# The second FFN's output product by Strassen's scheme, transposed, over two pairs of feature blocks at a time

## The chip, the cores and the metric

The kernel runs on one core of one Trainium2 chip. The metric is the device time of one execution in microseconds (us). Engines are named as in the profile: PE is the matmul engine and PEld its weight loads, DVE the vector engine, ACT the scalar engine, POOL GpSimd, SP the engine that issues the DMAs here.

## What is computed

Three steps in float32: banded attention, an FFN with a sigmoid gate on 2304 tokens, and a second FFN with separate gate and value products. Only the last one is changed.

```python
def _moe2_ref(x, w_gate, w_val, w_out):          # x: 2304 x 512
    g = x @ w_gate                               # 512 x 1536
    silu = g * (1.0 / (1.0 + np.exp(-g)))
    val = x @ w_val                              # 512 x 1536
    return (silu * val @ w_out).astype(np.float32)   # 1536 x 512
```

## The kernel before

Weights arrive as float64 words and are turned into two float32r halves, a high and a low part; activations are split the same way. Each product of 128x128 blocks is three matmuls (high by high, high by low, low by high).

**Order of the work.** The first 186 us or so are attention and the beginning of the first FFN, in an order written out by hand. Then the first FFN goes on over five blocks of tokens (`A_BLOCKS`) and 16 feature blocks, `h_part` and `y_part` in a loop over `idx`. Between those steps `advance(PACE[j])` runs some steps of `preparation`, which turns the second FFN's weights into the form in which they are used and writes them to scratch memory in HBM (`wscr`, `woscr`). The first FFN's result goes to `yscr` in HBM. The pools' slots and a scheduler with simulated time set the final order on each engine.

**The second FFN.** Tokens go in three groups `s` of 768, features in six pairs `p` of two 128-blocks: 18 pairs `q`, in the loop `for q in range(NQ)`. For each pair `gv_steps(q)` computes the gate (G) and the value (V) product by Strassen's scheme in Winograd's form: the matrices are cut in two by two quarters, and seven products of quarters (numbered 1 to 7) take the place of eight. A product (`product`) is 6 matmuls of 384 columns, and three PSUM banks collect them for each of G and V: `sx` takes products 1, 6, 7, 4 on top of each other, `sy` product 2, `sz` 5 and then 3. After 1, 5 and 6 ACT copies the bank (`keep_copy`, tile pc), after 2, 3 and 7 DVE adds a kept copy (`add`, tile c). `gate` then makes one quarter of silu(g)*v: tanh on ACT, two DVE operations, a copy to the high part on ACT and a subtraction for the low part on DVE (tile p).

`o_part(q, i)` multiplies tile i of 128 tokens of this result with the 256 rows of w_out that belong to the pair: 6 matmuls of 512 columns, of which the token tile is the stationary side, six such parts for a pair. The partial sums go to six accumulators in SBUF, by ACT for the first pair of a token group and by DVE (`acc`) for the others. The parts of pair q-1 run among the last products of pair q. `load_weights` brings the next pair's weights from scratch; its DMAs are issued by SP in order, each when the buffer it writes has been read for the last time. `y_steps` makes the seven sums of quarters of the activations for the next token group (tiles yr and ya), over the last two pairs of the group before, into the other one of two sets of buffers.

Of the kernel before, what the change touches and what calls it, by code (L numbers as in the profile page):

```python
# [26 lines left out]
PACE = {0: 1.4, 2: 2.0, 3: 2.2, 4: 2.3}  # L27

PAUSE = 77

PACE_LATE = 0.6
# [3 lines left out]
LATER = 2.5  # L35

SUPER = 6

O_ORDER = 3, 4, 5, 0, 1, 2

A_BLOCKS = (4, 2, 4, 4, 4)
# [40 lines left out]
def attention_two_ffn(ctx: ExitStack, tc: tile.TileContext, q, k, v, w_in, w_out, w_gate, w_val, w_out2, yscr, wscr, woscr, out):  # L82
# [9 lines left out]
    DM = out.shape[1]  # L92
# [25 lines left out]
    wpool = ctx.enter_context(tc.tile_pool(name="w", bufs=1, reuse_waits="tile"))  # L118
    cvp = ctx.enter_context(tc.tile_pool(name="cv", bufs=2))
# [114 lines left out]

    def fetch(slot, unit):

        m, p, h = unit
        pool, tag = slot()
        if m == "O":
            raw = pool.tile([P, 512, 2], U32, tag=tag, name="raw")  # L240
            src = w_out2[(2 * p + h) * P : (2 * p + h + 1) * P, :].bitcast(U32)
            nc.sync.dma_start(out=raw.rearrange("p c w -> p (c w)"), in_=src)
            return raw
        raw = pool.tile([P, 2, 2, P, 2], U32, tag=tag, name="raw")
        w = w_gate if m == "G" else w_val
        for f in range(2):
            src = w[2 * p + f].bitcast(U32).rearrange("p (a b c) -> p a b c", a=2, b=2)[:, :, h, :]
            nc.sync.dma_start(out=raw[:, f].rearrange("p a c w -> p a (c w)"), in_=src)
        return raw.rearrange("p f a c w -> p (f a c) w")

    def prepare(slot, raw, fetch_next, unit):

        m, p, h = unit
        cs = cvp.tile([P, 8, P], F32, tag="cv", name="cs")
        yield from fraction(raw, cs)
        fetch_next()
        if m == "O":
            pool, tag = slot()
            t = pool.tile([P, 1, 2, 512], F32R, tag=tag, name="wo")
            halves(t, slice(0, 1), cs.rearrange("p s c -> p (s c)")[:, :512].unsqueeze(1))  # L260
            nc.sync.dma_start(out=woscr[p][:, h * 1024 : (h + 1) * 1024], in_=flat(t))
            yield
            return
# [11 lines left out]
        at = wscr[p, "GV".index(m)]  # L275
        pool, tag = slot()
        wa = pool.tile([P, 4, 2, P], F32R, tag=tag, name="wa")
# [5 lines left out]
        wb = cvp.tile([P, 3, 2, P], F32R, tag="cv", name="wb")  # L283
# [317 lines left out]
    def y_part(j, f):  # L601
# [14 lines left out]
        for kk in range(KD):  # L616
            if j == len(a_blocks) - 1 and kk:
                yt = wpool.tile([P, TMAX * P], F32, tag=f"w{O_SLOTS - 1 + kk}", name="yt")
            else:
                yt = yo.tile([P, TMAX * P], F32, tag="yt", name="yt")  # L620
# [17 lines left out]
    def y_steps(s, tile_of):  # L638
# [3 lines left out]
        def quarter(i, j):  # L642
            t = yrp.tile([P, 2, HT], F32, tag="yr", name="yr")
# [13 lines left out]
        b11, b12, b22 = quarter(0, 0), quarter(0, 1), quarter(1, 1)  # L657
        split(1, b11)
        minus(b11, b12, b11)
        minus(b12, b22, b12)  # L660
# [3 lines left out]
        split(7, b12)  # L664
        b21 = quarter(1, 0)
        yield
        split(2, b21)
        split(6, b11)
        yield
        split(3, b22)  # L670
        minus(b11, b21, b11)
# [346 lines left out]
    for i in O_ORDER:  # L1018
        o_part(NQ - 1, i)
# [44 lines left out]
```

## Time and profile before

| what | value |
|---|---|
| median of 3 runs | 938.6 us (938.53 to 939.38) |
| the profiled execution's own time | 937.2 us |
| its span, first to last instruction | 935.4 us |
| PE busy | 916.7 us, 98% |
| DVE busy | 649.0 us, 69% |
| ACT busy | 422.0 us, 45% |
| second FFN, from its first matmul | from 517.4 us to the end |
| mean granted clock of TensorE | 0.994 |

The span is what the trace covers; 1.8 us of the execution's time lie outside it. Busy shares are averages over stages that differ; the second FFN is the stage that is changed most.

### The profile page before, as it was taken

How to read it: one execution, taken by the hardware profiler on the slowest of the kernel's cores; microseconds unless marked ns; L12 is line 12 of the kernel's file. 1: busy time of each engine (PE TensorE's matmuls, PEld its weight loads, DVE VectorE, ACT ScalarE, POOL GpSimd, SP SyncE). 2: the span in 40 equal slices, each digit the busy share in tenths (PEclk: the TensorE clock that was granted, in tenths of full speed). 3: DMA queues.
4: the chain of work that ended last, by engine and by line, in shares of the span. 5: the costliest groups of instructions: out<-in, count | busy, mean ns of one | idle time of the engine just before them, and what ended most of it. 6: DMA issues, size and time to landing. Idle time of an engine off the chain costs nothing.

```text
span 935.4 us, 15014 instructions
## 1 busy us (share of the span) xinstructions
PE 916.7 (98%) x5464; PEld 788.6 (84%) x5464; DVE 649.0 (69%) x1558; ACT 422.0 (45%) x968; POOL 123.6 (13%) x221
## 2 busy tenths in 40 slices
PE   6899999999999999999999999999999999999998
PEld 4577898787778877788888999999999999999996
DVE  7898797756876668757696567577545577545555
ACT  5565565643654446534454453344343343342321
POOL 4744004512331023300000000000000000000000
PEclk9899999999999999999999999999999999999999
DMA  8953202425543355435579488667765666766641
GB/s 319 358 200 134 93 13 62 151 93 166 176 150 128 126 195 192 139 108 191 196 267 325 166 333 322 226 211 265 265 209 203 208 255 220 275 213 216 212 151 67
DMA packets 62473, 182.38 MB, mean 195 GB/s; under 512 B 6080, under 2 KB 28096, under 8 KB 55488
## 3 DMA queue, kind: packets, MB, share of 16 engines
q1 hardware_dynamic: 62400, 181.43, 55.1%
q8 instruction: 43, 0.70, 0.3%
q14 instruction: 30, 0.25, 0.1%
HBM read 142.61 MB, written 38.80 MB: 194 GB/s over the span
## 4 chain that ended last, share of the span: by engine, by line
PE 86%; DVE 6%; DMA 3%; ACT 2%; POOL 1%; issue 1%; SPq 0%; DVEq 0%; POOLq 0%; ACTq 0%
PE sx L695 16%; PE o L765 16%; PE sz L695 8%; PE hp L561 6%; PE y L561 6%; PE hp L563 6%; PE y L563 6%; PE hp L562 6%; PE y L562 6%; PE sy L695 4%; PE xb L514 2%; PE sb L361 2%; PE pt L453 1%; DMA y_scratch<-yt 1%; DVE wraw L194 1%; POOL prob L421 1%
## 5 line engine op out<-in xcount | busy, mean ns | idle before, releaser
L695 PE MATMUL sx<-ya,wg 128*128 128x384 f32 x864 | 172.6, 336 | 0.0
L765 PE MATMUL o<-wo,p 128*128 128x512 f32 x648 | 158.9, 391 | 0.0
L695 PEld LDWEIGHTS sx<-ya,wg 128*128 128x128 f32 x864 | 153.1, 188 | 5.5 <-issue 0.3
L765 PEld LDWEIGHTS o<-wo,p 128*128 128x128 f32 x648 | 120.8, 188 | 21.4
L561 PE MATMUL hp<-xh,wt 128*128 128x512 f32 (+1 forms) x320 | 121.0, 378 | 0.5 <-DVE th L584 0.4
L563 PE MATMUL hp<-xh,wt 128*128 128x512 f32 (+1 forms) x320 | 118.1, 370 | 0.0
L562 PE MATMUL hp<-xl,wt 128*128 128x512 f32 (+1 forms) x320 | 118.0, 369 | 0.0
L562 PE MATMUL y<-gl,wt 128*128 128x512 f32 (+1 forms) x320 | 116.8, 371 | 0.5 <-DVE gl L592 0.5
L563 PE MATMUL y<-gh,wt 128*128 128x512 f32 (+1 forms) x320 | 117.0, 371 | 0.0
L561 PE MATMUL y<-gh,wt 128*128 128x512 f32 (+1 forms) x320 | 111.2, 377 | 0.2 <-DVE stat L386 0.2
L421 POOL TENSOR_SCALAR prob<-prob,stat 128x128 f32<-128x128 f32 x144 | 68.9, 498 | 204.4 <-DVE sb L331 55.7
L695 PE MATMUL sz<-ya,wg 128*128 128x384 f32 x432 | 84.1, 335 | 0.0
L592 DVE TENSOR_TENSOR gl<-th,gh 128x512 fp32r<-128x512 f32 (+1 forms) x80 | 52.4, 659 | 44.7 <-ACT gh L590 44.3
L590 ACT ACTIVATE gh<-th 128x512 fp32r<-128x512 f32 (+1 forms) x80 | 46.7, 586 | 78.5 <-PE y L563 55.2
L774 DVE SCALAR_TENSOR_TENSOR acc<-o,acc 128x512 f32<-128x512 f32 x90 | 61.4, 688 | 25.1 <-PE o L765 23.9
L695 PEld LDWEIGHTS sz<-ya,wg 128*128 128x128 f32 x432 | 75.8, 188 | 0.2
L716 DVE TENSOR_TENSOR c<-sy,pc 128x384 f32<-128x384 f32 x36 | 20.1, 558 | 79.5 <-PE sy L695 75.3
L561 PEld LDWEIGHTS hp<-xh,wt 128*128 128x128 f32 x320 | 60.4, 189 | 13.6 <-issue 1.6
L402 ACT ACTIVATE prob<-prob,stat 128x128 f32<-128x128 f32 x144 | 56.2, 392 | 34.4 <-DVE stat L386 34.3
L563 PEld LDWEIGHTS y<-gh,wt 128*128 128x128 f32 x320 | 60.3, 188 | 11.2 <-issue 1.0
L562 PEld LDWEIGHTS y<-gl,wt 128*128 128x128 f32 x320 | 60.3, 189 | 10.9 <-DVE gl L592 0.9
L563 PEld LDWEIGHTS hp<-xh,wt 128*128 128x128 f32 x320 | 60.2, 188 | 10.6
(90 smaller groups left out, 1385.6 us busy)
## 6 DMA issues: line engine op xcount, KB each, us to landing
wg<-w_scratch SPq DMA_DIRECT2D x36, 1024.0 KB, 6.9
wg<-w_scratch SPq DMA_DIRECT2D x36, 768.0 KB, 5.2
wo<-wo_scratch SPq DMA_DIRECT2D x18, 1024.0 KB, 6.9
w_scratch<-wa SPq DMA_DIRECT2D x24, 512.0 KB, 2.7
w_scratch<-wb SPq DMA_DIRECT2D x24, 384.0 KB, 3.5
wraw<-in_moe_w_in SPq DMA_DIRECT2D x16, 512.0 KB, 6.7
wraw<-in_moe_w_out SPq DMA_DIRECT2D x16, 512.0 KB, 7.3
raw<-in_moe_w_gate SPq DMA_DIRECT2D x24, 256.0 KB, 3.3
```

The costliest lines, as they stand in the source:

```text
L361: nc.tensor.matmul(out=sb[e][c : c + size, (i % 2) * 256 + lo : (i % 2) * 256 + hi], lhsT=u["q"][rows, i * P + c : i * P + c + size], rhs= ...
L402: nc.scalar.activation(out=prob[:, x], in_=prob[:, x], func=AF.Exp, bias=stat[:, 0, x : x + 1], scale=-1.0, accum_out=stat[:, 1, x : x + 1],)
L421: (nc.vector if (j, hp, g) in NORM_ON_VECTOR else nc.gpsimd).tensor_scalar(out=prob[:, x], in0=prob[:, x], scalar1=stat[:, 3, x : x + 1], ...
L561: nc.tensor.matmul(out=out_ap, lhsT=whi, rhs=xhi, start=start, stop=False)
L562: nc.tensor.matmul(out=out_ap, lhsT=whi, rhs=xlo, start=False, stop=False)
L563: nc.tensor.matmul(out=out_ap, lhsT=wlo, rhs=xhi, start=False, stop=stop)
L590: a = nc.scalar.activation(out=gh[:, :m], in_=th[:, :m], func=AF.Copy)
L592: d = nc.vector.tensor_tensor(out=gl[:, :m], in0=th[:, :m], in1=gh[:, :m].bitcast(F32), op=ALU.subtract)
L695: nc.tensor.matmul(out=bank_[:, :HT], lhsT=w[:, kk, at, a, :], rhs=y[:, b, kk, :], start=start and kk == 0 and n == 0, stop=kk == 1 and n ...
L716: marks["d"] = nc.vector.tensor_tensor(out=t, in0=b[:, :HT], in1=kept[m, k], op=ALU.add).ins
L765: nc.tensor.matmul(out=o, lhsT=ph[:, a, c], rhs=w[:, f, b, :], start=f == 0 and n == 0, stop=f == 1 and n == 2)
L774: nc.vector.scalar_tensor_tensor(out=acc, in0=o, scalar=0.5, in1=acc, op0=ALU.mult, op1=ALU.add)
```

## The change

**The output product.** `o_part` goes. `o_steps(q)` computes the output transposed (512 output rows by tokens; the host turns it back), with the weights as the stationary side and the gated activations moving. A group is two pairs, thus 512 features. For a group there are two calls, one for each `half` of the output rows, run during the two pairs after the group (the last group's two calls run at the end, interleaved). A call is again Strassen's seven products over three banks `ox`, `oy`, `oz`; a product is 6 matmuls of 384 columns, 3 with the pieces of each of the group's pairs. After each of the seven, the bank is added to an accumulator (DVE), or copied to it in a token group's first group of pairs for four of them (ACT).

**The pieces.** `pieces_of` takes the place of the end of `gate`: from the four gated quarters it makes the seven operands, four more subtractions on DVE, and splits each of the seven in a high and a low part (tile p, 24 buffers), where before there were four such splits.

**The weights of the output product** are prepared as those of G and V are: 8 steps for a unit in place of 4, seven quarters in place of four, and `load_weights` fetches two pieces of 1024 and 768 KB for each pair, where before it was one of 1024 KB. G's and V's weights move to a pool `kept` that shares its slots with four of the first FFN's weights.

**Around it.** `PACE` is higher, preparation rests at `REST`, goes on in the second FFN from its third pair at 0.8 steps a product, and the activations' sums for the next token group (`y_steps`) are made within one pair, into a single set of buffers.

```diff
-PACE = {0: 1.4, 2: 2.0, 3: 2.2, 4: 2.3}
-PAUSE = 77
-PACE_LATE = 0.6
+PACE = {0: 2.0, 2: 2.4, 3: 2.5, 4: 2.7}
+REST = 74
+LATE, PACE_LATE = 2, 0.8
...
+KEPT = 3, 5, 4, 6
+P_BUFS = 24
+O_STEPS = 1, 5, 6, 2, 7, 3, 4
...
-    def y_steps(s, tile_of):
+    def y_steps(s, tile_of, slot):
...
     def product(q, m, i, bank_, start):
         half, at = W_OF[i]
-        w, y = w2[q, m, half], y2[q // NP2, i]
+        w = w2[q, m, half]
         for kk in range(2):
             for n, (a, b) in enumerate(((0, 0), (0, 1), (1, 0))):
                 nc.tensor.matmul(
                     out=bank_[:, :HT],
                     lhsT=w[:, kk, at, a, :],
-                    rhs=y[:, b, kk, :],
+                    rhs=p2[2 * (q // 2 - 1) + kk, i][:, b, :] if m == "O" else y2[q // NP2, i][:, b, kk, :],
...
+        def split(i, src):
+            t = pp.tile([P, 2, HT], F32R, tag="p", name="p2", bufs=P_BUFS)
+            nc.scalar.activation(out=t[:, 0], in_=src, func=AF.Copy)
+            nc.vector.tensor_tensor(out=t[:, 1], in0=src, in1=t[:, 0].bitcast(F32), op=ALU.subtract)
+            p2[q, i] = t
...
+        def pieces_of(i):
+            gate(i)
+            if i == (0, 0):
+                split(1, b[i])
+            elif i == (1, 1):
+                split(3, b[i])
+            elif i == (0, 1):
+                b11, b12, b22 = b[0, 0], b[i], b[1, 1]
+                minus(b11, b12, b11)
+                split(5, b11)
+                minus(b12, b22, b12)
+                split(7, b12)
+                minus(b22, b22, b11)
+                split(6, b22)
+            else:
+                split(2, b[i])
+                minus(b[i], b[i], b[1, 1])
+                split(4, b[i])
...
-        for pair in ((1, 5), (2, 6), (3,), (7,), (4,)):
+        for pair in ((1, 5), (2, 6), (7,), (3,), (4,)):
...
-    def o_part(q, i):
-        p, s = q % NP2, q // NP2
-        w = w2[q, "O", 0]
-        o = bank("o")
-        c = slice(i * P, (i + 1) * P)
-        for f in range(2):
-            ph = p2[q][f]
-            for n, (a, b) in enumerate(((0, 0), (0, 1), (1, 0))):
-                nc.tensor.matmul(
-                    out=o, lhsT=ph[:, a, c], rhs=w[:, f, b, :], start=f == 0 and n == 0, stop=f == 1 and n == 2
-                )
...
+    def o_steps(q):
+
+        banks = {}
+        g, half = q // 2 - 1, q % 2
+        s, first, last = g // 3, g % 3 == 0, g % 3 == 2
+        for i in O_STEPS:
+            x = {1: "x", 6: "x", 7: "x", 4: "x", 2: "y", 5: "z", 3: "z"}[i]
+            new = x not in banks
+            if new:
+                banks[x] = bank("o" + x)
+            t = banks[x]
+            product(q, "O", i, t, new)
+            a, b = {1: (0, 0), 2: (0, 0), 6: (0, 1), 3: (0, 1), 5: (1, 1), 7: (1, 1), 4: (1, 0)}[i]
+            if first and i in (1, 5, 6, 4):
+                acc = pp.tile([P, HT], F32, tag=f"acc{half}{a}{b}", name="acc")
+                o2[half, a, b] = acc
+                nc.scalar.activation(out=acc, in_=t[:, :HT], func=AF.Copy, scale=0.5)
+            else:
+                acc = o2[half, a, b]
+                nc.vector.scalar_tensor_tensor(out=acc, in0=t[:, :HT], scalar=0.5, in1=acc, op0=ALU.mult, op1=ALU.add)
+            if last and i in (2, 3, 7, 4):
+                rows, cols = (2 * a + half) * P, s * SUPER * P + b * HT
+                nc.sync.dma_start(out=out[rows : rows + P, cols : cols + HT], in_=acc)
+            yield i
...
     for q in range(NQ):
         s, p = divmod(q, NP2)
-        if s + 1 < NS and p == NP2 - 2:
...
+        if s + 1 < NS and p == NP2 - 1:
+            pieces[s + 1] = y_steps(s + 1, piece, slot)
+        behind = o_steps(q) if q > 1 else iter(())
         for n, (m, i) in enumerate(gv_steps(q)):
...
+            if n % 2:
+                done = next(behind, None)
+                if done and q < NQ - 1:
+                    last_weights(q, done)
...
+    for _ in zip(o_steps(NQ), o_steps(NQ + 1)):
+        pass
```

**On PE**, in a pair near the end, before (tiles sx, sy, sz are the banks of G and V, o the bank of the output product, p_8884 and p_8885 the two feature blocks of the pair before):

```order
L695 MATMUL sz<-ya,wg 128x384 x12
L695 MATMUL sx<-ya,wg 128x384 x6
L765 MATMUL o<-wo,p_8884 128x512 x3
L765 MATMUL o<-wo,p_8885 128x512 x2
L695 MATMUL sx<-ya,wg 128x384 x6
L765 MATMUL o<-wo,p_8885 128x512
L765 MATMUL o<-wo,p_8884 128x512 x3
L765 MATMUL o<-wo,p_8885 128x512 x3
```

The same place with the change (ox, oy and oz are the output product's banks, the two tiles p pieces of the group's two pairs):

```order
L710 MATMUL sx<-ya,wg 128x384 x6
L710 MATMUL sz<-ya,wg 128x384 x6
L710 MATMUL oz<-p_9029,wg 128x384 x3
L710 MATMUL oz<-p_9252,wg 128x384 x3
L710 MATMUL sy<-ya,wg 128x384 x6
L710 MATMUL sx<-ya,wg 128x384 x6
L710 MATMUL ox<-p_9037,wg 128x384 x3
L710 MATMUL ox<-p_9260,wg 128x384 x3
```

The output product's matmuls now have the shape of G's and V's and stand after each second product of these, where before they had 512 columns and stood together in the second part of the pair.

**On DVE**, the end of a quiet pair before (c is `add`, th `gate`, p the low part, acc the output's accumulation):

```order
L716 TENSOR_TENSOR c_8980<-sz,pc 128x384
L725 SCALAR_TENSOR_TENSOR th_8982<-th_8982,c_8972 128x384
L716 TENSOR_TENSOR c_8994<-sx,pc 128x384
L726 TENSOR_TENSOR th_8982<-th_8982,c_8980 128x384
L725 SCALAR_TENSOR_TENSOR th_9004<-th_9004,c_8994 128x384
L729 TENSOR_TENSOR p_8884<-th_8982,p_8884 128x384
```

With the change (L734 is `minus` on the gated quarters, L739 the low part of a piece):

```order
L747 TENSOR_TENSOR th_9467<-th_9467,c_9465 128x384
L746 SCALAR_TENSOR_TENSOR th_9504<-th_9504,sx 128x384
L734 TENSOR_TENSOR th_9394<-th_9467,th_9394 128x384
L747 TENSOR_TENSOR th_9504<-th_9504,sx 128x384
L734 TENSOR_TENSOR th_9467<-th_9437,th_9467 128x384
L816 SCALAR_TENSOR_TENSOR acc<-ox,acc 128x384
L739 TENSOR_TENSOR p_9472<-th_9394,p_9472 128x384
L734 TENSOR_TENSOR th_9437<-th_9437,th_9394 128x384
L739 TENSOR_TENSOR p_9476<-th_9467,p_9476 128x384
```

Four L734 and three more L739 have come in for each pair.

**On SP**, before, the fourth quarter of the activations for the second token group (yr_6570) stands ahead of the second halves of the weights of pair 5:

```order
L684 DMA wg_6487<-w_scratch 128x2048 [waits DMAHW5_49,PE_49]
L684 DMA wg_6512<-w_scratch 128x2048 [waits DMAHW7_49,PE_49]
L645 DMA yr_6570<-y_scratch 128x2x384 [waits DVE_49]
L684 DMA wg_6578<-w_scratch 128x1536 [waits DMAHW6_49,DMAHW0_49,PE_49]
L684 DMA wg_6592<-w_scratch 128x1536 [waits DMAHW1_49,PE_49]
```

With the change it is issued in pair 5 (yr_6874), behind G's second half for pair 6 (wg_7022), which waits for the last product of G in pair 5:

```order
L699 DMA wg_6876<-w_scratch 128x2048 [waits DMAHW1_49,PE_49]
L699 DMA wg_6921<-w_scratch 128x2048 [waits PE_49]
L699 DMA wg_6931<-wo_scratch 128x2048 [waits PE_49]
L699 DMA wg_7022<-w_scratch 128x1536 [waits DMAHW4_49,PE_49]
L643 DMA yr_6874<-y_scratch 128x2x384 [waits DMAHW5_49,DVE_49]
L699 DMA wg_7050<-wo_scratch 128x1536 [waits DMAHW6_49,PE_49]
```

DVE meets this quarter behind the last gate of pair 5 (th2_7030):

```order
L747 TENSOR_TENSOR th2_7030<-th2_7030,sx_6811 128x384 [waits DVE_49]
L653 TENSOR_TENSOR yr_6821<-yr_6874,yr_6821 128x768 [waits DMAHW5_49,DVE_49]
L649 TENSOR_TENSOR ya_6904<-yr_6874,ya_6904 128x768 [waits Activation_49]
L734 TENSOR_TENSOR th2_6894<-th2_6993,th2_6894 128x384 [waits DVE_49]
L649 TENSOR_TENSOR ya_6982<-yr_6821,ya_6982 128x768 [waits Activation_49]
```

So the wait for the fourth quarter has moved from the next-to-last pair of a token group to the border of two groups, and pieces of pair 5 (L734) stand behind it on DVE.

## Rows read from the trace of the kernel before

**Rows 1.** The page's head, busy times, and the chain's share by engine.

```profile
span 935.4 us, 15014 instructions
...
PE 916.7 (98%) x5464; PEld 788.6 (84%) x5464; DVE 649.0 (69%) x1558; ACT 422.0 (45%) x968; POOL 123.6 (13%) x221
...
PE 86%; DVE 6%; DMA 3%; ACT 2%; POOL 1%; issue 1%; SPq 0%; DVEq 0%; POOLq 0%; ACTq 0%
```

**Rows 2.** Windows: us, busy time of each engine, PEclk, DMA share, GB/s.

```profile
350.00:375.00 25.00, 25.00 (x212) 18.70 (x215) 21.25 (x74) 15.46 (x51) 7.95 (x19) 1.00 0.51 179
...
475.00:500.00 25.00, 25.00 (x112) 20.67 (x112) 22.13 (x43) 12.66 (x23) 0.00 (x0) 1.00 0.76 270
...
517.40:935.40 418.00, 414.10 (x2173) 386.30 (x2171) 258.83 (x463) 151.88 (x299) 0.00 (x0) 1.00 0.64 225
```

**Rows 3.** The chain that ended last, 880 us to the end: start, us, what.

```profile
902.67 1.04 PE sx L695 x6
...
920.19 11.36 PE o L765 x50
...
931.57 0.69 DVE acc L774
```

**Rows 4.** Waits of PEld from 500 us on: us in total, times, longest.

```profile
PEld sx L695 <- issue: 0.3, 1, 0.3
```

**Rows 5.** The second FFN's window for the line L695 alone (PE, PEld).

```profile
517.40:935.40 418.00, 273.77 (x1512) 264.29 (x1511) 1.00 0.64 225
```

**Rows 6.** The same window for the line L765 alone.

```profile
517.40:935.40 418.00, 158.95 (x648) 120.79 (x648) 1.00 0.64 225
```

**Rows 7.** The line L695: duration in ns, least, median, most.

```profile
L695 PEld LDWEIGHTS sx<-ya,wg x864: 187/188/190, 517.2 to 919.7; 128*128 128x128 f32 x173
```

**Rows 8.** DVE's groups by shape in the second FFN: busy us, mean ns.

```profile
L774 DVE SCALAR_TENSOR_TENSOR acc<-o,acc 128x512 f32<-128x512 f32 x90 | 61.4, 688 | 25.1 <-PE o L765 23.9
L729 DVE TENSOR_TENSOR p<-th,p 128x384 fp32r<-128x384 f32 x72 | 39.9, 554 | 15.4 <-ACT p L728 15.4
...
L651 DVE TENSOR_TENSOR ya<-yr,ya 128x768 fp32r<-128x768 f32 x14 | 13.3, 950 | 0.0
```

**Rows 9.** DVE's timeline, 541 to 590 us: start, duration, instruction, idle before it.

```profile
557.06 0.55 DVE L725 SCALAR_TENSOR_TENSOR th<-th,sx 128x384 f32<-128x384 f32 x1 [2.18 <-ACT th L724]
557.71 0.55 DVE L726 TENSOR_TENSOR th<-th,sx 128x384 f32<-128x384 f32 x1
...
569.38 0.55 DVE L716 TENSOR_TENSOR c<-sz,pc 128x384 f32<-128x384 f32 x1
569.85 0.55 DVE L725 SCALAR_TENSOR_TENSOR th<-th,c 128x384 f32<-128x384 f32 x1
570.32 0.55 DVE L716 TENSOR_TENSOR c<-sx,pc 128x384 f32<-128x384 f32 x1
...
573.12 0.68 DVE L774 SCALAR_TENSOR_TENSOR acc<-o,acc 128x512 f32<-128x512 f32 x1
573.72 0.68 DVE L230 TENSOR_TENSOR wo<-cs,wo 128x512 fp32r<-128x512 f32 x1
```

**Rows 10.** ACT's groups by shape in the second FFN.

```profile
L728 ACT ACTIVATE p<-th 128x384 fp32r<-128x384 f32 x72 | 37.6, 522 | 63.2 <-DVE th L726 63.0
L711 ACT ACTIVATE pc<-sx 128x384 f32<-128x384 f32 x72 | 35.1, 488 | 64.1 <-PE sx L695 63.7
```

**Rows 11.** Windows of 6 us in the second FFN, columns as in Rows 2.

```profile
529.00:535.00 6.00, 5.96 (x34) 5.67 (x34) 5.80 (x13) 3.12 (x6) 0.00 (x0) 1.00 0.89 289
...
541.00:547.00 6.00, 6.00 (x34) 5.72 (x33) 4.94 (x12) 3.83 (x9) 0.00 (x0) 1.00 1.02 403
547.00:553.00 6.00, 6.00 (x31) 5.30 (x30) 4.37 (x10) 3.13 (x6) 0.00 (x0) 1.00 0.88 366
```

**Rows 12.** DMA issues: engine, count, KB each, median us to landing.

```profile
wg<-w_scratch SPq DMA_DIRECT2D x36, 1024.0 KB, 6.9
...
yr<-y_scratch SPq DMA_DIRECT2D x12, 384.0 KB, 5.2
```

More of the change, by code (lines that the diff above doesn't have):

```diff
@@ L91, in attention_two_ffn @@
     S = 576
-    DM = out.shape[1]
+    DM = out.shape[0]
     KD = DM // P
@@ L274, in prepare @@
         yield
[L275 to L277 removed]
+        at, h = scratch(*unit)
+        wa = slot([P, 4, 2, P], F32R, "wa")
         halves(wa, slice(0, 2), cs[:, 0:2])
@@ L663, in y_steps @@
         minus(b11, b22, b11)
-        split(7, b12)
-        b21 = quarter(1, 0)
-        yield
[L667 to L671, printed above, removed]
+        if s == 0:
+            split(7, b12)
+            b21 = quarter(1, 0)
+            yield
+            split(2, b21)
+            split(6, b11)
+            yield
+            split(3, b22)
+        else:
+            b21 = quarter(1, 0)
+            yield
+            split(2, b21)
+            yield
+            split(6, b11)
+            yield
+            split(7, b12)
+            yield
+            split(3, b22)
+        minus(b11, b21, b11)
+        yield
         split(4, b11)
@@ L706, in gv_steps @@
         banks, kept, c = {}, {}, {}
-        p2[q] = [wpool.tile([P, 2, 2 * HT], F32R, tag=f"w{12 + 2 * (q % 2) + f}", name="p2") for f in range(2)]
         def keep_copy(m, i, b):
@@ L917, in attention_two_ffn, with slot, fetch_next, prepared @@
     bctx = ExitStack()
-    todo = [(m, p, h) for p in range(NP2) for m in "GVO" for h in range(2)]
-    todo.sort(key=lambda u: u[1] + (LATER if u[0] == "O" else 0))
-    closed, turn = [], [0]
-    def slot():
-        if not closed:
-            return att, "er"
-        turn[0] += 1
-        return wpool, f"w{(turn[0] - 1) % O_SLOTS}"
-    def preparation():
-        raws = []
-        def fetch_next():
-            if len(raws) < len(todo):
-                raws.append(fetch(slot, todo[len(raws)]))
-        fetch_next()
-        yield
-        for i, u in enumerate(todo):
-            yield from prepare(slot, raws[i], fetch_next, u)
+    todo = [(m, p, h) for m in "GVO" for p in range(NP2) for h in range(2)]
+    todo.sort(key=lambda u: u[1] if u[0] != "O" else 4.5 if u[1] < 4 else 6)
+    where, turn, rest = [att], [0], [False]
+    def slot(shape, dtype, name):
+        pool, tag = where[0], "er"
+        if pool is att and name in ("cs", "wb"):
+            pool, tag = cvp, "cv"
+        elif pool is wpool:
+            turn[0] += 1
+            tag = f"w{7 + (turn[0] - 1) % O_SLOTS}"
+        return pool.tile(shape, dtype, tag=tag, name=name, bufs=2 if pool in (att, cvp) else 1 if pool is wpool else 4)
+    ready, busy = {}, [False]
+    def preparation():
+        for i, u in enumerate(todo):
+            def fetch_next(i=i + 1):
+                if i < len(todo) and not rest[0]:
+                    ready[i] = fetch(slot, todo[i])
+            while i not in ready:
+                fetch_next(i)
+                yield
+            busy[0] = True
+            yield from prepare(slot, ready.pop(i), fetch_next, u)
+            busy[0] = False
+            made.add(u)
+    def prepared(*wanted):
+        while not made.issuperset(wanted):
+            in_order(work)
+    made = set()
     work, owed = preparation(), [0.0]
@@ L952, in advance, with settle @@
             in_order(work)
+    def settle(pool):
+        rest[0] = True
+        while busy[0] or ready:
+            in_order(work)
+        rest[0] = False
+        where[0] = pool
     for idx, (j, f) in enumerate(seq):
@@ L963, in attention_two_ffn @@
             split_next(w1, raw1, need)
+        if (j, f) == (na - 1, CLOSE - 2) or idx == REST:
+            rest[0] = True
         if (j, f) == (na - 1, CLOSE):
-            closed.append(True)
+            settle(wpool)
             attx.close()
```

159 lines of the change are left out of this document (72 added, 87 removed).

## Prediction, made before the changed kernel ran

> **What bounds the kernel now.** I read the page's shares first, then windows, the chain, PE's waits, and last DVE and the DMA queue in the stage that changes. The reader is to see in the page that PE is busy 98% of the span and makes up 86% of the chain [rows 1]. A busy PE alone doesn't show a bound, so the windows come next: from 517.4 us on, PE is busy 414.1 of 418.0 us while DVE has 258.8 and ACT 151.9 [rows 2], and PE's weight loads waited 0.3 us in all of it [rows 4]. The chain there is PE's two lines and nothing else until the last accumulation [rows 3]. So the second FFN lasts as long as its matmuls follow one another.
>
> The spacing of matmuls has to be read from start to start, since their durations overlap. Six matmuls of L695 (384 columns) take 1.04 us, 0.1734 each; 50 of L765 (512 columns) take 11.36 us, 0.2272 each [rows 3]. There are 1512 of the first and 648 of the second [rows 5, 6]: 262.2 + 147.2 = 409.4 us. What is left of 414.1 is matmuls of the first FFN that run in between. The prices explain the stage to 1%.
>
> **PE's part of the change.** 648 matmuls of L765 go: 147.2 us. 18 calls of 7 products of 6 matmuls come, 756 in L695's very shape: 756 x 0.1734 = 131.1 us. That is 16.1 us less. A pair costs 84 x 0.1734 = 14.57 us without output product (pairs 0 and 1 now) and 126 x 0.1734 = 21.85 us with it.
>
> This holds only if columns set the spacing, not the weight loads, of which there are 108 more. A load lasts 188 ns, longer than the 173 ns spacing [rows 3, 7], so loads must overlap each other; and the two spacings differ by 53.8 ns for 128 columns, which is 128 cycles at the granted 2.4 GHz (clock 1.00 in rows 2). Columns set it. The Trainium skill (Perfetto Trace Analysis, Identifying the Most-Contended Engine) wants the matmul engine's distance to its limit judged by the share of weight-load time and not by matmul busy time. Here that share is 386.3 of 418.0, 92%; by it the change would add 108 x 0.188 = 20.3 us in place of taking 16.1. It is a rival below.
>
> **DVE.** Per pair, four more subtractions and three more low parts come, and accumulations are seven of 384 columns in place of six of 512. A quiet pair has 6 adds, 8 gate operations, 7 low parts, 4 subtractions, 7 accumulations: 32 instructions. Their durations are 0.55 us, but back to back they start 0.47 us apart, and 0.60 for 512 columns of 0.69 [rows 8, 9]: 0.13 for each 128 columns, which gives 0.86 for 768 (duration 0.95). A quiet pair then costs 15.0 us of PE's 21.85; pairs 0 and 1, without accumulations, 11.8 of 14.57. Preparation adds about five units in pairs 1 to 5 (ten instructions each, some 3.8 us by the same prices), and pair 5 makes all 7 splits and 4 differences of 768 columns for the next token group, 9.5 us. Counted by the order, pairs 0 to 6 cost DVE 11.8, 12.2, 18.2, 17.9, 20.6, 25.3 and 17.4: 123.4 us, against 2 x 14.57 + 5 x 21.85 = 138.4 on PE. Only pair 5 is over, by 3.5 us. With whole durations the sum is 145.9, over PE's by 7.5. I take the first, since rows 9 show it, and keep the second for the range. An instruction that uses the one just before it starts 0.65 after it [rows 9]; some eight of these in a pair add 1 to 1.5 us, which every pair but 4 and 5 has to spare.
>
> The Trainium skill (VectorE: DVE Perf Modes, The DRAIN you can't avoid) says that the next operation doesn't start until the pipeline is empty, unless it isn't held back. By the first half of that, 145.9 us holds; the trace has the next start 0.08 us ahead of an operation's end. It stands as a rival too.
>
> **The border of token groups.** Before, the fourth quarter of the activations is issued a pair earlier. Now SP issues it behind G's second half of weights, thus when the last G product of pair 5 has ended (T). It lands 5.2 us later by its median, up to 2 us more for the 768 KB ahead of it at 403 GB/s [rows 11, 12]. DVE comes to its subtraction when V's last product, 19 matmuls behind, is gated: T + 3.3 + 0.7. So DVE waits 1.2 to 3.2 us, behind which three subtractions and low parts of pair 5 and the next pair's adds stand, and it is 3.5 us late from pair 5 anyway. PE has some six products (6 us) that need none of it. I take 3 us of PE's time; bounds 0 and 6.7 (3.5 + 3.2). At the second border all four quarters are issued pairs earlier, and pairs 11 and 12 cost DVE 20.9 and 17.9: nothing.
>
> **DMA.** A pair's weights grow from 4.7 to 5.5 MB (3 times 1024 and 768 KB, [rows 12]). With preparation and activations, pairs 2 to 5 issue 30.9 MB in 87.4 us, 354 GB/s. The trace shows 403 and 366 GB/s without a wait of PE, and 289 in a window whose DMA share was 0.89 [rows 11]. A weight load lands in 6.9 us and is issued about ten products (10.4 us) ahead. I take 1 us; bounds 0 and, were 289 all there is, 30.9/0.289 - 87.4 = 19.5.
>
> **What is hidden.** ACT gets 7 splits in place of 4: 6 copies, 4 tanh, 7 splits at 0.49 to 0.52 [rows 10] are 8.7 us of a pair. In the first FFN 47 more DVE instructions of preparation, some 18 us, spread over 330 us; DVE was busy 21.3 and 22.1 of 25 us in the fullest windows without a wait of PE [rows 2], and 2 us more fit. Cost 0; where the cover is gone, 1 us. At the start of the second FFN the first bank copies wait for a write of y to land, while PE has four products (4.2 us) ahead: 0. At the end 84 output matmuls stand alone, one accumulation of 0.47 for each product of 1.04, and pair 17's last pieces are due after products of pair 16: 0; the last accumulation is 0.13 shorter.
>
> **Sum.** -16.1 + 3 + 1 = -12.1. The profiled execution took 937.2, thus 925.1; the median of the runs is 1.4 above it: **926.5 us**.
>
> **Rivals.**
> - DVE becomes the bound in pairs 2 to 6. For it: pair 5 is over in any case, and in-order waits on ACT come on top. Against it: rows 9. At whole durations PE loses 7.5, with the wait at the border (3) and DMA (1) 11.5: 938.6 - 16.1 + 11.5 = 934; with DVE idle 6% of that stretch as well, 9 us more, 943. It turns the sign where DVE needs 138.4 + 16.1 = 154.5 us for these pairs. 0.15.
> - Slower by one mechanism: the DMA queue. In pairs 2 to 5 weights arrive late when writes, raw weights and loads share it. At 289 GB/s PE waits 19.5: 938.6 - 16.1 + 19.5 + 3 = 945. The gain is gone below 30.9/(87.4 + 13.1) = 307 GB/s. For it: the 289 GB/s window at a share of 0.89; against it: 403 two windows later. 0.10. The Trainium skill (DMA: Bandwidth & Descriptors, Where 436 GB/s comes from) puts the HBM side's limit at about 358 GB/s; by that these pairs just fit, and the trace was above it for 12 us.
> - The weight loads bind, so the change doesn't shorten PE but adds 108 loads of 188 ns [rows 7], 20.3 us: 938.6 + 20.3 + 4 = 963. Against it: the spacings above. 0.02.
>
> **How the numbers follow.** Forecast, PE bound with small losses: 922 to 932, 0.73. The range reaches from no loss at all (922.5) over the forecast and most of the DVE case to 937; outside lie the DMA case and DVE's worst third, under 0.2 together. About 0.2%, 1.9 us, is what a measurement of this kernel can tell from none. Faster: 0.73 and 0.09 of the DVE case, 0.82. Slower: 0.07 of DMA, 0.02 of DVE, 0.02 of the loads, 0.11. The rest, 0.07, is the same.
>
> **What would show it.** Right: the output product's matmuls 0.173 us apart; PE without waits from 517 us but around pair 5's end, some 116 us into the stage (2 x 14.57 + 4 x 21.85); DVE starts 0.47 apart there. Wrong: PE waiting for DVE in pairs 2 to 4 (DVE's price), for weight DMAs with a share near 1 (the queue), spacing near 0.19 (loads), or PE waits in the first FFN, where I priced 47 instructions at nothing.

## The result, and the profile after

The changed kernel takes 927.2 us (median of 4 runs, 925.7 to 930.4) against 939.0 of before (4 runs, 938.5 to 939.7): a ratio of 0.988, 95% interval 0.985 to 0.991. The forecast was 926.5. Its profiled execution took 926.7 us. From here on "the stage" is the second FFN, from PE's first matmul of `sx` to the end of the last accumulation.

The page's head and its busy times after ([rows 1] before), and the window of the second FFN (us, PE, PEld, DVE, ACT, POOL, PEclk, DMA share, GB/s; [rows 2] before):

```profile
span 924.9 us, 15685 instructions
...
PE 901.5 (97%) x5572; PEld 798.5 (86%) x5572; DVE 717.1 (78%) x1768; ACT 453.6 (49%) x1052; POOL 123.2 (13%) x221
```

```profile
520.10:924.90 404.80, 398.18 (x2281) 396.34 (x2280) 314.93 (x634) 177.21 (x369) 0.00 (x0) 1.00 0.78 279
```

PE is still the busy engine, 398.2 of 404.8 us; its weight loads are at 396.3, and they don't bind (run `o_cols256`). DVE went from 258.8 to 314.9 us. The stage lasts from 520.14 to 921.96 us, 401.8 us, where before it was 517.43 to 932.26, 414.8 us: 13.0 us less. PE's timeline where it begins, before and after (the ends are the last accumulations, in [rows 3] and in the chain below):

```profile
517.43 1.20 PE L695 MATMUL sx<-ya,wg 128*128 128x384 f32 x6
...
520.14 1.20 PE L710 MATMUL sx<-ya,wg 128*128 128x384 f32 x6
```

All of PE's waits in the stage, in us, times, longest (before, the 0.3 us of a weight load in [rows 4] were all), and below them the two at the border of token groups in PE's timeline (start, duration, idle time before it):

```profile
PE sx L710 <- DMA wg<-w_scratch: 1.4, 1, 1.4
PE ox L710 <- DMA wg<-wo_scratch: 1.1, 1, 1.1
PE sz L710 <- DMA wg<-w_scratch: 0.6, 1, 0.6
```

```profile
667.14 1.28 PE L710 MATMUL sz<-ya,wg 128*128 128x384 f32 x6 [0.59 <-DMA wg<-w_scratch]
669.54 1.31 PE L710 MATMUL ox<-p,wg 128*128 128x384 f32 x6 [1.13 <-DMA wg<-wo_scratch]
```

Every wait of PE is for weights, none for DVE: 3.1 us in three places, the first (1.4 us) at 539 us, where pair 1 begins. The 16.1 us that PE was to gain, less these 3.1, are the 13.0 of the stage; what PE gained without waits is measured further down (`hold_split`).

The chain after, in a quiet pair and at the end ([rows 3] before):

```profile
576.80 1.04 PE sz L710 x6
577.85 1.06 PE ox L710 x6
...
917.20 4.18 PE ox L710 x24
...
921.40 0.56 DVE acc L816
```

Six output matmuls take 1.06 us here and six of G or V 1.04. The end is as counted: PE alone until 921.4, then one accumulation.

DVE where pair 5 ends (start, duration):

```profile
646.97 0.54 DVE L739 TENSOR_TENSOR p<-th,p 128x384 fp32r<-128x384 f32 x1
647.43 0.54 DVE L747 TENSOR_TENSOR th<-th,sx 128x384 f32<-128x384 f32 x1
647.90 0.94 DVE L653 TENSOR_TENSOR yr<-yr 128x768 f32<-128x768 f32 x1
648.77 0.94 DVE L649 TENSOR_TENSOR ya<-yr,ya 128x768 fp32r<-128x768 f32 x1
```

DVE starts 0.47 us apart, 0.87 for 768 columns, as priced. It comes to the fourth quarter (L653 at 647.90) without a wait: SP issued G's second half at 640.31 (T of the prediction) and the quarter at 640.73, which landed 5.0 us later, and DVE came at T + 7.6, where the prediction's count without lateness had T + 4.0. The Trainium skill (VectorE: DVE Perf Modes, The DRAIN you can't avoid) says that the next operation does not start until the pipeline is empty, and that one which is not held starts earlier; the second is what these rows show, 0.07 us of overlap each time.

### The profile page after: what moved, and what is told of

Read it like the earlier page. It is cut to its first block, busy times and chain, and to the rows that moved or that the text cites. A ratio compares the mean times of both kernels' runs of the same rounds, so it can differ in the third digit from the quotient of the medians.

```text
span 924.9 us, 15685 instructions
## 1 busy us (share of the span) xinstructions
PE 901.5 (97%) x5572; PEld 798.5 (86%) x5572; DVE 717.1 (78%) x1768; ACT 453.6 (49%) x1052; POOL 123.2 (13%) x221
## 4 chain that ended last, share of the span: by engine, by line
PE 82%; DVE 8%; DMA 5%; ACT 2%; POOL 1%; issue 1%; SPq 0%; DVEq 0%; POOLq 0%; ACTq 0%
PE sx L710 15%; PE ox L710 8%; PE sz L710 8%; PE hp L559 6%; PE y L559 6%; PE y L561 6%; PE y L560 6%; PE hp L561 6%; PE hp L560 6%; PE sy L710 4%; PE oz L710 4%; PE oy L710 2%; PE xb L512 2%; PE sb L359 2%; PE pt L451 1%; DMA y_scratch<-yt 1%
## 5 line engine op out<-in xcount | busy, mean ns | idle before, releaser
L710 PE MATMUL ox<-p,wg 128*128 128x384 f32 x432 | 89.6, 337 | 1.1 <-DMA wg<-wo_scratch 1.1
L710 PE MATMUL sz<-ya,wg 128*128 128x384 f32 x432 | 88.3, 336 | 0.6 <-DMA wg<-w_scratch 0.6
L739 DVE TENSOR_TENSOR p<-th,p 128x384 fp32r<-128x384 f32 x126 | 68.1, 552 | 23.7 <-ACT p L738 23.0
L738 ACT ACTIVATE p<-th 128x384 fp32r<-128x384 f32 x126 | 63.6, 520 | 35.7 <-DVE th L734 25.6
L710 PEld LDWEIGHTS ox<-p,wg 128*128 128x128 f32 x432 | 76.4, 188 | 1.5 <-DMA wg<-wo_scratch 1.4
L559 PEld LDWEIGHTS hp<-xh,wt 128*128 128x128 f32 x320 | 60.3, 189 | 14.9 <-issue 1.6
L561 PEld LDWEIGHTS y<-gh,wt 128*128 128x128 f32 x320 | 60.3, 188 | 11.1 <-issue 1.0
L559 PEld LDWEIGHTS y<-gh,wt 128*128 128x128 f32 x320 | 57.3, 188 | 14.5 <-issue 2.6
L560 PEld LDWEIGHTS y<-gl,wt 128*128 128x128 f32 x320 | 60.4, 189 | 10.6 <-DVE gl L590 0.9
```

The lines of the kernel that those rows point to most:

```text
L559: nc.tensor.matmul(out=out_ap, lhsT=whi, rhs=xhi, start=start, stop=False)
L560: nc.tensor.matmul(out=out_ap, lhsT=whi, rhs=xlo, start=False, stop=False)
L561: nc.tensor.matmul(out=out_ap, lhsT=wlo, rhs=xhi, start=False, stop=stop)
L710: nc.tensor.matmul(out=bank_[:, :HT], lhsT=w[:, kk, at, a, :], rhs=p2[2 * (q // 2 - 1) + kk, i][:, b, :] if m == "O" else y2[q // NP2, i][ ...
L738: nc.scalar.activation(out=t[:, 0], in_=src, func=AF.Copy)
L739: nc.vector.tensor_tensor(out=t[:, 1], in0=src, in1=t[:, 0].bitcast(F32), op=ALU.subtract)
```

## The experiments

**What repeats.** The kernel after and the kernel before, unaltered, profiled a second time.

> The changed kernel once more, unaltered. It tells what repeats: in the first profile the second FFN began at 520.1 us, 2.7 us later than before, and PE waited 3.1 us for weights (1.4 at 539 us, 0.6 and 1.1 at 667 to 670 us). If the 2.7 us come from the denser preparation, the second FFN begins at 519.5 to 520.5 us again; if they were chance, anywhere from 517 to 520. The three waits for weights come back if they are a matter of the order on SP. Time 926 to 928 us.

> The kernel before, unaltered, profiled once more. Its first profile came from an execution of 937.2 us, the fastest of all so far, and its second FFN began at 517.4 us; in five profiles of changed kernels it began at 519.2 to 520.4 us. Theory chance (the first profile of before was a quick one, the change cost the first FFN next to nothing): it begins at 518.5 us or later. Rival preparation (the change delays the first FFN by some 2 us): it begins at 517 to 518 us again.

`again`: 928.0 us (926.3 to 928.6), ratio 0.989 (0.987 to 0.991). Its waits:

```profile
PE sx L710 <- DMA wg<-w_scratch: 1.7, 1, 1.7
PE ox L710 <- DMA wg<-wo_scratch: 1.1, 1, 1.1
PE sz L710 <- DMA wg<-w_scratch: 0.7, 1, 0.7
```

The three waits come back at the same places, 3.5 us. `before_again` took 939.7 us, and PE's timeline shows its second FFN begin here:

```profile
519.67 1.20 PE L695 MATMUL sx<-ya,wg 128*128 128x384 f32 x6
```

`again` began it at 519.38, the other profiles of changed kernels at 518.5 to 521.0. So the 517.4 us of the first profile of before was a quick execution, and most of the 2.7 us by which the changed kernel seemed to lose time ahead of the second FFN was chance: theory chance holds by its mark (518.5 us or later). That the 47 more instructions of preparation cost nothing isn't shown: the twelve profiles of changed kernels begin the second FFN at 519.9 us on the mean and the two of before at 518.6, which leaves room for some 1 us. The stage itself repeats: 415.1 us before, 402.2 after.

**Do columns or weight loads set the spacing?** The output's matmuls with a third of their columns left out; its accumulations have 256 columns too, and each output write is two DMAs.

```diff
-                    out=bank_[:, :HT],
+                    out=bank_[:, : 256 if m == "O" else HT],
-                    rhs=p2[2 * (q // 2 - 1) + kk, i][:, b, :] if m == "O" else ...
+                    rhs=p2[2 * (q // 2 - 1) + kk, i][:, b, :256] if m == "O" else ...
```

> Leaves out a third of the tokens of the output product: its matmuls and accumulations have 256 columns in place of 384, the number of matmuls and weight loads stays. Theory columns (columns set the spacing of matmuls): 0.1734 - 128 x 0.4167 ns = 0.120 us apart, 756 x 0.0533 = 40 us less, 887 us, up to 8 us more where weights arrive late because pairs get shorter by 2.2 us. Rival loads (a weight load of 188 ns, two of them overlapping, bounds the spacing somewhere above 0.120): less is gained, and if the loads bound it already now, nothing.

One run: 906.6 us, where 887, or up to 8 more, was expected. Its chain:

```profile
700.06 0.71 PE oy L710 x6
...
700.95 1.04 PE sx L710 x6
701.98 0.71 PE ox L710 x6
```

0.71 us for six, 0.118 each, with as many loads as before: columns set the spacing, and 0.173 was not near a limit of the loads. 756 x (0.176 - 0.118) = 44 us left PE, but the stage (521.04 to 898.93 us) is only 23.9 us shorter than the changed kernel's. PE's waits took 12 more us: they are 15 us in all, the longest 5.4 us for `wg<-wo_scratch` at 671 us; 10 of the 15 are for weights, 5 for ACT and DVE. Three stretches of 3.4 us at half clock took 5 us; for some 3 us there is no account. As soon as PE gets much shorter, the bound moves to the transfers and, at the border of token groups, to DVE and ACT.

**Is DVE near its limit?** Three kernels: the four differences of gated quarters left out, and the low part of four pieces computed twice, or four times (`range(4` in `dve_plus12`).

```diff
-                minus(b11, b12, b11)
                 split(5, b11)
-                minus(b12, b22, b12)
                 split(7, b12)
-                minus(b22, b22, b11)
                 split(6, b22)
...
-                minus(b[i], b[i], b[1, 1])
                 split(4, b[i])
```

```diff
-            nc.vector.tensor_tensor(out=t[:, 1], in0=src, ...)
+            for _ in range(2 if q > 1 and i in (1, 3, 2, 7) else 1):
+                nc.vector.tensor_tensor(out=t[:, 1], in0=src, ...)
```

> Leaves out the four differences of gated quarters in each pair, so that the seven pieces are split from plain quarters: DVE has 72 instructions of 384 columns less, 1.9 us a pair, 34 us in all. Theory PE (matmuls set the time and DVE lies beside them): no change within 1 us, 926 to 928 us, the waits for weights stay. Rival DVE (DVE held PE in pairs 2 to 6, directly or by late pieces): 5 pairs by 1.9 us, up to 9.4 us less, 917 to 922 us.

> In each pair from the third on, the low part of four pieces is computed twice: four more DVE instructions of 384 columns, the result unaltered. My sum: pairs 0 to 6 cost DVE 123.4 + 5 x 4 x 0.47 = 132.8 us against 138.4 of PE, quiet pairs 18 against 21.85, so no change within 2 us, 926 to 929 us, and no wait of PE for DVE over 1 us in sum. Rival durations (an instruction costs DVE its whole 0.55 us): 145.9 + 11 = 156.9 us against 138.4, 18 us slower, some 945 us.

> As the one before with the low part of four pieces computed four times: twelve more DVE instructions in each pair from the third on. My sum: pairs 0 to 6 cost DVE 123.4 + 5 x 12 x 0.47 = 151.6 us against 138.4, 13 us over; a quiet pair 15.0 + 1.2 + 5.6 = 21.8 against 21.85, just even; pairs 11 and 12 26.5 and 23.5, up to 6 over. So 13 to 25 us slower, 940 to 952 us, with PE's waits for DVE in pairs 4 to 7. Rival durations: 178.9 against 138.4 there, and 24.2 against 21.85 in each quiet pair, some 60 us slower, 985 us. Rival reserve (DVE has far more slack than counted): no change.

`dve_minus4`: 930.1 us (928.6 to 931.8), ratio 0.991 (0.989 to 0.992). With 34 us less of DVE (72 x 0.47) it is 2 to 3 us slower by the medians, and its stage 5.0 us longer in the profile, which is of its slowest execution (931.8 us); neither theory expected that. Without PE's waits and what half clock took, its stage is 398.2 us, the changed kernel's 398.7: less work for DVE gave 0.5 us back, where rival DVE wanted up to 9.4. That refutes it. Why it is slower stands in PE's timeline and in windows around the first of these waits:

```profile
539.78 2.17 PE L710 MATMUL sx<-ya,wg 128*128 128x384 f32 x6 [1.91 <-DMA wg<-w_scratch]
...
672.14 1.53 PE L710 MATMUL ox<-p,wg 128*128 128x384 f32 x6 [3.25 <-DMA wg<-wo_scratch]
```

```profile
536.00:538.00 2.00, 1.88 (x11) 1.56 (x9) 2.00 (x5) 0.90 (x2) 0.00 (x0) 1.00 1.01 421
538.00:540.00 2.00, 0.21 (x1) 0.22 (x2) 2.00 (x5) 1.24 (x3) 0.00 (x0) 0.99 1.04 422
540.00:542.00 2.00, 2.00 (x7) 2.00 (x7) 2.00 (x6) 1.46 (x4) 0.00 (x0) 0.50 0.95 392
542.00:544.00 2.00, 2.00 (x9) 2.00 (x9) 0.94 (x2) 0.76 (x2) 0.00 (x0) 0.66 0.84 347
```

The waits for weights grew to 5.2 us, and after each of the two the granted clock is 0.50, the 1.2 GHz level, for 3.4 us (here 2.0 + 2 x 0.34/0.5 us), in which PE does about half its work (7 and 9 matmuls in 2 us, where the changed kernel has 13 and 14 from 540 to 544 us): 1.7 us more each time. The first of the two waits need not come from the edit: at the same place `again` has 1.7 us, and `dve_plus4`, which alters nothing before pair 2, has 1.9.

`dve_plus4`: 935.5 us (932.4 to 938.1), ratio 0.997 (0.995 to 0.998), some 8 us slower than the changed kernel. All of PE's waits:

```profile
PE ox L710 <- DMA wg<-wo_scratch: 4.4, 2, 3.8
PE sx L710 <- DMA wg<-w_scratch: 3.3, 2, 1.9
PE sz L710 <- DMA wg<-w_scratch: 1.1, 1, 1.1
PE oy L710 <- DVE c L730: 0.4, 1, 0.4
```

PE waited 0.4 us for DVE, so DVE kept up, as the sum of starts said, and the whole durations did not hold (18 us). But the time rose all the same, by weights. In SP's timeline the output product's weights for pair 7 (`wg<-wo_scratch`), for which PE waits 3.8 us, are issued 6.4 us later; first the changed kernel, then this one:

```profile
658.91 0.32 SPq L699 DMA_DIRECT2D wg<-w_scratch  x1
659.33 0.38 SPq L699 DMA_DIRECT2D wg<-wo_scratch  x1
661.26 0.34 SPq L819 DMA_DIRECT2D out<-acc  x1
```

```profile
659.46 0.33 SPq L699 DMA_DIRECT2D wg<-w_scratch  x1
662.52 0.35 SPq L820 DMA_DIRECT2D out<-acc  x1
665.30 0.32 SPq L699 DMA_DIRECT2D wg<-w_scratch  x1
665.71 0.38 SPq L699 DMA_DIRECT2D wg<-wo_scratch  x1
```

The order on SP is another, and one could take the output write ahead of the load for the cause. But PE's timeline shows when the buffer that the load writes is read for the last time, by two matmuls of product 2 (`oy`) in pair 6. In the changed kernel, in `dve_plus4` and in `second_queue_plus4` (below):

```profile
658.72 0.51 PE L710 MATMUL oy<-p,wg 128*128 128x384 f32 x2
...
665.11 0.51 PE L710 MATMUL oy<-p,wg 128*128 128x384 f32 x2
...
671.91 0.51 PE L715 MATMUL oy<-p,wg 128*128 128x384 f32 x2
```

In all three the load is issued 0.1 to 0.2 us after these two end (659.33, 665.71 and 672.59), in the third with no output write on SP at all. So it waited for its buffer. With a few more DVE instructions these two matmuls stand four products further back in PE's order, the buffer comes free 6.4 us later, and so does the load.

`dve_plus12`: 963.5 us (961.7 to 965.8), ratio 1.026 (1.024 to 1.028), beyond the 940 to 952 expected. PE waits 9.8 us for DVE and ACT, 7.5 of them in pairs 5 to 7, where my sum put DVE 13 us over by the end of pair 6; 14.6 us are for weights, and some 24 us run at half clock. So the sum of DVE's starts gives DVE's own excess roughly, and what follows from it more than doubles the price.

**Where do the late weights come from?** Four kernels. `hold_both` queues two groups of transfers later on SP (`held(n)` puts a DMA behind the last weights of pair n); `no_o_preparation` leaves out those of the output product's preparation; `second_queue` lets POOL issue all but the weight loads; `second_queue_plus4` is that with the added DVE instructions of `dve_plus4`.

```diff
+        with held(1 if m == "O" and q == 2 else None):
+            loads[q] = nc.sync.dma_start(...).ins
...
+            with held(9 if s == 2 else None):
                 nc.sync.dma_start(out=t, in_=yscr[:, 2 * i : 2 * i + 2, a : a + HT])
```

```diff
-    todo = [(m, p, h) for m in "GVO" for p in range(NP2) for h in range(2)]
+    todo = [(m, p, h) for m in "GV" for p in range(NP2) for h in range(2)]
```

```diff
+    def queue():
+        return nc.gpsimd if where[0] is pools.get("pp") else nc.sync
...
-                nc.sync.dma_start(out=out[rows : rows + P, cols : cols + HT], in_=acc)
+                queue().dma_start(out=out[rows : rows + P, cols : cols + HT], in_=acc)
```

> Two groups of DMAs are queued later on SP: the output product's weights for pair 2 behind the last weights of pair 1, and the four quarters of the third token group behind the weights of pair 9. Theory order (the waits for weights come from what stands ahead of them on SP and in the queue): the waits at 539 and at 667 to 670 us go, 3.1 us in all, and the time is 923 to 925 us. Rival bandwidth (pairs 1 to 6 move more than the queue carries): the waits come back elsewhere in pairs 1 to 7 with 2 us or more in sum, time 926 to 928 us.

> Leaves out the preparation of the output product's weights; its products read the gate product's prepared weights in their place, so PE does the same work. Theory preparation (the 2.7 us lost ahead of the second FFN come from the denser preparation): the second FFN begins at 517 to 518 us, the waits at 667 to 670 us go with the raw weights and writes that are left out, time 922 to 924 us. Rival (the 2.7 us have another cause): it begins at 519.5 us or later, time 925 to 927 us. If DVE bounded pairs 2 to 6, the 12 units with some 4 us of DVE each that are left out would give back more than 5 us there, time below 922 us.

> In the second FFN the DMAs that can wait for DVE or for other transfers (raw weights, prepared weights to scratch, quarters of the activations, output) are issued by POOL, which is idle there; SP issues the weight loads alone. Theory order on SP (weights come late since they are issued behind DMAs that wait for DVE or for a transfer): PE's waits at 667 to 670 us fall from 1.7 us to under 0.5, the one at 539 us stays, time 925 to 927 us. Rival capacity (the DMA engines are full from 655 to 672 us, whoever issues): the waits at 667 to 670 us stay, 927 to 928 us.

> The two queues of the run before and the four more DVE instructions a pair of dve_plus4 (the low part of four pieces computed twice) together. dve_plus4 cost 7.5 us with only 0.4 us of PE waiting for DVE; its waits were for weights, one of 3.8 us with 6.8 us of half clock behind it. Theory order on SP (late DVE held SP, and SP the weights): the two queues take that away, 927 to 930 us, with no wait of PE for weights over 2 us around 660 to 680 us. Rival DVE or capacity (DVE itself is too late there, or the engines are full): 933 to 936 us as dve_plus4.

`hold_both`: 926.1 us (925.2 to 930.3), ratio 0.988 (0.986 to 0.990). Its waits in PE's timeline:

```profile
535.13 1.28 PE L717 MATMUL sx<-ya,wg 128*128 128x384 f32 x6 [0.29 <-DMA wg<-w_scratch]
553.39 1.31 PE L717 MATMUL sx<-ya,wg 128*128 128x384 f32 x6 [1.37 <-DMA wg<-w_scratch]
...
665.77 1.28 PE L717 MATMUL sz<-ya,wg 128*128 128x384 f32 x6 [0.46 <-DMA wg<-w_scratch]
```

The border's waits fell from 1.7 to 0.5 and the one at the start of pair 1 to 0.3; but a new one came at pair 2, whose first weights were issued behind the 1.75 MB that had been held. By the marks set, the rival came out (2.1 us of waits, 926.1 us); what the rows show is that the place of a transfer matters, and that moving a burst moves the wait.

`no_o_preparation`: 926.0 us (925.3 to 927.5), ratio 0.987 (0.985 to 0.988). The border is free of waits, but two of 1.9 and 1.0 us stand at 538 and 543 us: with the raw weights gone, quarters of the activations (four of 384 KB) were issued among pair 1's weights. Its second FFN began at 519.2, between the marks of the two theories: no gain ahead of it that can be told. With 41 us less of DVE (676.3 against 717.1 us busy) the time is that of the changed kernel, which speaks against DVE as the bound once more.

`second_queue`: 934.0 us (932.9 to 934.1), ratio 0.995 (0.994 to 0.996), 7 us slower than the changed kernel. PE waits 5.4 us, all for weights. Windows at the border:

```profile
655.00:660.00 5.00, 5.00 (x30) 5.00 (x30) 4.46 (x10) 2.96 (x7) 2.53 (x4) 1.00 0.23 71
660.00:665.00 5.00, 5.00 (x31) 5.00 (x30) 5.00 (x12) 1.39 (x3) 0.76 (x2) 1.00 0.99 343
665.00:670.00 5.00, 3.17 (x14) 2.85 (x13) 4.19 (x9) 1.92 (x4) 1.83 (x3) 0.84 1.02 423
670.00:675.00 5.00, 4.66 (x22) 4.33 (x21) 1.79 (x4) 0.90 (x2) 0.00 (x0) 0.82 1.01 408
```

Theory order on SP falls. With SP free for them the weights came no sooner: the border's waits are 2.3 us (1.8 and 0.4) in place of 1.7, and the one at the start of pair 1 grew to 2.9 us, where POOL issued two raw loads (at 528.24 and 532.80 us) that the changed kernel issues later. At the border quarters, writes and weights met: 71 GB/s in one stretch of 5 us, then 343, 423 and 408 with the engines full (a share of 0.99 to 1.02) in the next three, and the clock down behind the wait. `second_queue_plus4`: 942.1 us (939.6 to 945.2), ratio 1.004 (1.002 to 1.006), PE waiting 10.6 us for weights; taking the issue from SP cured nothing there either, as the load that was late in `dve_plus4` waits for PE's last read of its buffer. POOL's queue is no remedy; the page lists it as `software_dynamic` and SP's as `hardware_dynamic`, so a second queue of SP's kind is not tested.

**Spreading the bursts.** `both_queues` is `second_queue` with both groups held back, the output's weights for pair 2 in two steps; `hold_split` is the same without the second queue.

```diff
+        with held(((1, "V", 1), (2, "V", 0))[half] if m == "O" and q == 2 else None):
+            loads[q, m, half] = nc.sync.dma_start(...).ins
...
+            with held((9, "V", 1) if s == 2 else None):
                 nc.sync.dma_start(out=t, in_=yscr[:, 2 * i : 2 * i + 2, a : a + HT])
```

> second_queue with two DMAs held back on SP: the output product's weights for pair 2 in two steps, the first half behind pair 1's weights, the second behind the first of pair 2's, and the quarters of the third token group behind the weights of pair 9. In hold_both the wait at 539 us fell to 0.3, and a new one of 1.4 came at 553 us behind both halves. Theory order: all waits for weights together under 1 us, time 923.5 to 926 us. Rival capacity: 1.5 us or more remain, 926 to 928 us.

> One queue as in the changed kernel; held back on SP are the output product's weights for pair 2 (first half behind pair 1's weights, second half behind the first of pair 2's) and the quarters of the third token group (behind the weights of pair 9). Taking the issue from SP did not shorten the waits (second_queue), holding transfers back did, so the theory is now bursts: the DMA engines carry some 410 GB/s, and a weight load waits while more is issued ahead of it than that carries. Theory bursts: waits for weights under 1 us in sum (0.3 at 535 us, 0.5 at 666 us), none over 1 us, second FFN some 399.5 to 400.5 us, time 924.5 to 926.5 us. Rival sum (pairs 1 to 6 as a whole carry too much): waits of 2 us or more come back elsewhere, time 926.5 to 928 us.

`both_queues`: 927.8 us (927.0 to 929.5), ratio 0.989 (0.988 to 0.990). Waits for weights fell to 0.2 us, but from 634 to 653 us PE now waits 2.1 us for DVE and ACT; the time is that of the changed kernel. `hold_split`: 926.3 us (923.6 to 927.4), ratio 0.987 (0.986 to 0.989). Where its stage begins and ends, and all that PE waits for in it:

```profile
519.52 1.20 PE L717 MATMUL sx<-ya,wg 128*128 128x384 f32 x6
...
918.38 0.56 DVE L823 SCALAR_TENSOR_TENSOR acc<-ox,acc 128x384 f32<-128x384 f32 x1 [0.49 <-PE ox L717]
```

```profile
PE sx L717 <- DMA wg<-w_scratch: 0.2, 1, 0.2
```

Its stage runs from 519.52 to 918.94, 399.4 us, 2.4 less than the changed kernel's, with 0.2 in place of 3.1 us of waits: theory bursts holds. The runs' intervals overlap, so of the time alone the gain isn't shown; the profile, one of each kernel, shows it.

**The account.** With 399.2 us for a stage without a wait (`hold_split` less its 0.2), the stage of each kernel with all its columns is that, plus its waits, plus half of its time at half clock (worked out from windows, each for (1 - PEclk)/0.5 of its length), to 1 us in all but the last:

| kernel | waits of PE | at half clock | sum | stage measured |
|---|---|---|---|---|
| changed kernel | 3.1 | 0 | 402.3 | 401.8 |
| changed kernel, `again` | 3.5 | 0 | 402.7 | 402.2 |
| hold_both | 2.1 | 0 | 401.3 | 401.1 |
| both_queues | 2.4 | 0 | 401.6 | 402.2 |
| no_o_preparation | 3.0 | 0 | 402.2 | 401.6 |
| dve_minus4 | 5.2 | 6.8 | 407.8 | 406.8 |
| dve_plus4 | 9.2 | 6.8 | 411.8 | 411.2 |
| second_queue | 5.4 | 6.8 | 408.0 | 407.5 |
| second_queue_plus4 | 11.7 | 10 | 415.9 | 416.0 |
| dve_plus12 | 24.4 | 24 | 435.6 | 438.4 |

## Why the prediction was right

- **PE's part, -16.1 us:** right. `hold_split`, with no wait to speak of, has a stage 15.4 to 15.6 us shorter than the two of before. Both prices were a little low, and nearly cancel: the output's matmuls are 0.176 us apart in place of 0.1734 (1.06 us for six; 756 x 0.0026 = 2.0 us), and the old ones among other products 0.228 to 0.230 (14 in 3.19 us, 5 in 1.15) in place of 0.2272, 0.5 to 1.8 us.
- **Weight loads don't bind:** right; 0.118 us apart with 256 columns. The share of weight-load time, 98% of the stage now, told nothing of a limit.
- **DVE by its starts (123.4 us for pairs 0 to 6):** right. DVE was busy 122.5 us from 520.14 to 664.30, PE's pairs 0 to 6; PE never waited for it, and four more instructions a pair brought 0.4 us of waits.
- **The border, +3 us of PE waiting behind DVE:** wrong, 0. The step that failed is "So DVE waits 1.2 to 3.2 us, ... and it is 3.5 us late from pair 5 anyway": the two were added, but a DVE that comes 3.5 us late meets a quarter that has landed. It came 3.6 us later than the count without lateness and waited for nothing; PE's products ahead covered that. The cover is not wide: in `both_queues` PE waits 2.1 us for DVE and ACT here.
- **DMA, +1 us:** mis-sized; it is 3.1 (3.5 in `again`). I took it from the mean rate of pairs 2 to 5. The waits come from bursts of some 10 us: 1.4 us at the start of pair 1, outside the pairs that I had counted, and 1.7 at the border, where quarters for a group six pairs ahead and writes were issued among the weights. There the loads of 1 MB landed after 8.2 to 10.2 us (issues from 650 to 670 us), not the 6.9 that I set against ten products.
- **First FFN, transition and end at 0:** the end is right by the last rows of the chain, and PE waits for nothing from 520.1 to 537 us. The first FFN is open to some 1 us (`before_again`): the stage gained 13.0 us and in `again` 12.9, the medians 11.8 and 10.9.
- **The sum, -12.1 us:** the stage gave -13.0, since the 3 us of the border were not there and the 3.1 of DMA were nearly what the two terms had together. The medians differ by 11.8; `again` has 10.9 against its own runs of before. PE's part was reasoned and came out; that the whole comes within 1 us of the forecast is in part luck, since one term was 3 us too high and the other 2 too low.
- **Rivals:** DVE bound and loads are refuted. The DMA queue, as priced (19.5 us over four pairs), did not come, but its mechanism is the one that costs: waits for weights are 10 of 15 us in `o_cols256`, 8.8 of 9.2 in `dve_plus4` and all 5.4 in `second_queue`.

What stays open is, in part, what spreads the executions of one kernel over 4 us. Of the eight of the changed kernel, the four with a granted clock of 0.993 or 0.994 took 925.7 to 927.7 us and the four with 0.989 or 0.990 took 927.9 to 930.4, so more time at half clock goes with it; but `hold_split` has 925.5 us at 0.989 and 927.1 at 0.994, and where the clock fell is known for the profiled executions alone. Open is also why a few instructions on DVE give another order on PE and SP: that the order changed is read from the timelines.

## What to carry to other kernels

Where PE bounds a stage, price its change by start-to-start spacing in rows of the same shape, and then look for waits at the places where transfers bunch, over some 10 us and not over pairs: hold back what is not needed soon, rather than give it to POOL's queue. When a load is issued late, ask which matmul read its buffer last before blaming what stands ahead of it. A wait on PE can cost more than its length, so compare kernels by waits and granted clock before putting a difference down to the edit. When something is late, ask what it would have waited for if it had been in time: two delays of one instruction don't add up.

## What was unexpected of the hardware

- With every wait of PE of 2.5 us or more in the stage (2.47 in `o_cols256` is the shortest), the granted clock fell to the 1.2 GHz level, in the wait or within 1.2 us of its end, and stayed there for 3.4 to 6.8 us. Of those of 1.8 to 1.9 us, three were followed by it (1.91 us in `dve_minus4`, 1.83 in `second_queue`, 1.81 in `o_cols256`) and two were not (1.92 in `no_o_preparation` and in `dve_plus4`); none of 1.7 us or less was, but one of 1.6 us in `dve_plus12` close behind another of 3.3.
- The transfers ran at 399 to 424 GB/s from 655 to 669 us in the changed kernel, by windows of 3 to 5 us, with the DMA share at 0.97 to 1.06; `second_queue` had 423 in 5 us. The Trainium skill (HBM Reference, Specifications (TRN2)) gives some 358 GB/s for a core of a busy pair and about 425 for one that streams alone; these rows agree with the second. The prediction weighed the first, which did not bind here.
- In `second_queue` POOL was busy 0.54 to 0.73 us for each DMA that it issued.
